# First MLP of a fused attention and MLP kernel: the products with w_ch2 two tiles behind those with w_ch1 instead of one

## Chip, cores and metric

One core of one Trainium2 chip. The metric is the device time of one execution in microseconds (us), the median of three runs. TensorE is called PE in the views, its weight loads PEld, VectorE DVE, ScalarE ACT, GpSimd POOL; SP is the engine that issues most transfers.

## What is computed

Three stages follow each other, all in float32 on the outside. Batch 4, 8 heads, 576 positions, head width 64, model width 512:

```python
def _attn_ref(q, k, v, f):
    ...
    decay = cum[:, :, :, None] - cum[:, :, None, :]
    scores = np.where(causal, -1000000000.0, scores + decay)
    ...
    return np.matmul(attn, v).astype(np.float32)

def _moe_ref(x, g_ln, w_ch1, w_ch2):
    ...
    xn = (x - mu) / np.sqrt(var + 1e-06) * g_ln
    ch = np.maximum(xn @ w_ch1, 0.0) @ w_ch2
    return (x + ch).astype(np.float32)

def _moe2_ref(x, w_in, w_spatial, b_spatial, w_out):
    h = np.maximum(x @ w_in, 0.0)
    ...
    return (gated @ w_out).astype(np.float32)
```

The middle one is the first MLP: 512 columns to 2048 with `w_ch1`, a relu, and back to 512 with `w_ch2`. Its normalisation is over the 512 columns.

## The kernel before

The 2304 rows (4 x 576) are cut into nine blocks of 256. Blocks 0 to 7 come from attention, one after the other; block 8 gathers the last 64 positions of each batch element. The first MLP works through eight groups, called 0 to 7 here: groups 0 to 6 have one block each, group 7 has blocks 7 and 8 together, so its matmuls are 512 columns wide where the others have 256. Attention of later blocks, the normalisation of the next block, the conversion of weights from 64-bit words (groups 0 and 1) and the loading of the second MLP's weights (group 7, `load_m2`) are written between the MLP's steps by a list of events sorted by due time in `run`; a list scheduler then fixes each engine's order by priority and readiness, and on the chip every engine runs its list in that order.

One step of a group is one tile `j` of 128 of the 2048 hidden columns (`NF` = 16 tiles). It has these parts:

- the **first products** (line 652), `w_ch1` times the normalised rows, into a PSUM tile `ph`. Weights and rows are split into a high and a low half in 16 bits, so there are 4 x 3 = 12 matmuls per tile (4 in group 0, which runs in float32). `ph` has **two** buffers;
- the relu in two halves: ScalarE writes `hh` (line 657), then VectorE `hl` from `ph` and `hh` (line 661). Both have three buffers. `ph` is free for tile `j` + 2 when both have read it;
- the **second products** (line 637, function `second`), `w_ch2` times `hh` and `hl`, again 12 matmuls, which accumulate over all 16 tiles in two PSUM banks `acc` (in group 7 two more, `s2`, which some views call `s`). They are issued one step late: step `j` issues the first products of tile `j` and then the second products of tile `j` - 1, which `pend` holds.

After the last tile `acc` is scaled by VectorE (line 677) and added to `x2_d` in memory by GpSimd's transfers (line 681).

In attention a pair of heads has its score products on line 280 (line 373 in blocks 2 and 3), is made into 16-bit probabilities `P` by VectorE and ScalarE, is transposed by transfers (line 303, queue of SP) into `PT`, and comes back to TensorE in 30 products `av` with the values (line 436; line 398 in blocks 2 and 3). The normalisation of a block has two small products with a matrix of ones (line 557): of the sum `ls` for the mean and of the squares `sq` for the variance. Behind them VectorE scales `xT` (line 587), and `split` makes `xh` (ScalarE, line 613) and `xl` (VectorE, line 614), the right sides of the first products.

Of the kernel before, what the change touches and what calls it, by code (L numbers as in the profile page):

```python
# [22 lines left out]
NF = DFF // P  # L23
# [12 lines left out]
NARROW = 4  # L36
W8 = 1
RAWB = 2

BLOCKS = [(0, 0), (2, 0), (0, 1), (2, 1), (0, 2), (1, 2), (2, 2), (3, 2)]  # L40
EPS = 1e-6
# [29 lines left out]
def f32(ap):  # L71
    return ap.bitcast(F32)
# [7 lines left out]
class Kernel:  # L80
# [140 lines left out]
    def vnorm(self):  # L221
# [4 lines left out]
        for b in range(B + 1):  # L226
            t = self.st.tile([P, 4, DM], F32, tag="raw", name="vraw", bufs=RAWB)
            if b < B:
# [261 lines left out]
    def load_raw(self, j):  # L490
        nc = self.nc
        cs = slice(j * P, (j + 1) * P)
        raw = self.raw[j] = self.st.tile([P, 2 * DM], I64, tag="raw", name="raw", bufs=RAWB)
        nc.sync.dma_start(out=raw[:, :DM].rearrange("p (k f) -> p k f", k=NK), in_=self.moe_w_ch1[:, cs].rearrange("(k p) f -> p k f", p=P))
# [104 lines left out]
    def mlp(self, g, states, y):  # L599
        nc, mo = self.nc, self.mo  # L600
        n = len(states)
        W = n * TOK
        if g:
            xn = [[mo.tile([P, 2 * TOK], F16, tag=tag, name=tag, bufs=MB["xh"]) for tag in ("xh", "xl")] for _ in range(NK)]

        def split(i):

            x, c = states[i](), slice(i * TOK, (i + 1) * TOK)
            for t in range(NK):
                with self.tc.high_priority(1):  # L610
                    if g:
                        scale, (xh, xl) = self.gs[:, t : t + 1], xn[t]
                        nc.scalar.activation(xh[:, c], x[:, t, :], AF.Copy, scale=scale)  # L613
                        nc.vector.scalar_tensor_tensor(out=xl[:, c], in0=x[:, t, :], scalar=scale, in1=xh[:, c], op0=ALU.mult, op1=ALU.subtract)  # L614
                    else:
                        nc.scalar.activation(x[:, t, :], x[:, t, :], AF.Copy, scale=self.gT[:, t : t + 1])
            return x

        acc = self.accs(W)
        clear, seen = {}, set()  # L620

        def weight(j, c0, right):

            cs = slice(c0, c0 + P)
            if not g:
                return [(self.wt[:, j + 2, cs], right)]
            h, l = self.pair(j)
            rh, rl = right
            return [(l[:, cs], rh), (h[:, cs], rl), (h[:, cs], rh)]

        def second(j, hidden, last):
            for m in range(NK):

                bank = m if n > 1 else m // 2
                terms = weight(j, DM + m * P, hidden)
                for e, (a, b) in enumerate(terms):
                    ins = nc.tensor.matmul(acc[m], lhsT=a, rhs=b, start=bank not in clear, stop=last and e == len(terms) - 1, skip_group_check=True)  # L637
                    if bank not in clear:
                        clear[bank] = ins
                    elif m not in seen and not e:  # L640
                        self.after(ins, clear[bank])
                    seen.add(m)

        pend = None
        for i in range(n):
            x = split(i)
        for j in range(NF):
            ph = self.bank("ph")[:, :W]
            for k in range(NK):
                terms = weight(j, k * P, (xn[k][0][:, :W], xn[k][1][:, :W]) if g else x[:, k, :])  # L650
                for e, (a, b) in enumerate(terms):
                    nc.tensor.matmul(ph, lhsT=a, rhs=b, start=k == e == 0, stop=k == NK - 1 and e == len(terms) - 1)  # L652
            hh = mo.tile([P, 2 * TOK], F16, tag="hh", name="hh", bufs=MB["hh"])
            hl = mo.tile([P, 2 * TOK], F16, tag="hl", name="hl", bufs=MB["hh"])[:, :W] if g else None
            hh = hh[:, :W] if g else f32(hh)
            with self.tc.high_priority(1):
                relu = nc.scalar.activation(hh, ph, AF.Relu)  # L657
                if g < 2:
                    self.done.append(relu)
                if g:  # L660
                    nc.vector.scalar_tensor_tensor(out=hl, in0=ph, scalar=0.0, in1=hh, op0=ALU.max, op1=ALU.subtract)  # L661
            if pend is not None:
                second(*pend)
            pend = (j, (hh, hl) if g else hh, j == NF - 1)
            yield
        second(*pend)
        c = GROUPS[g][0] * TOK
        for i in reversed(range(n)):

            t = mo.tile([P, NK, TOK], F32, tag="xT", name="t", bufs=MB["xT"])  # L670
            for m in range(NK):
                a = acc[m][:, i * TOK : (i + 1) * TOK]
                with self.tc.high_priority(1):
                    if n > 1 and m % 2:
                        nc.scalar.activation(t[:, m], a, AF.Copy, scale=self.und)
                    elif g:
                        nc.vector.tensor_scalar(out=t[:, m], in0=a, scalar1=self.und, scalar2=None, op0=ALU.mult)
                    else:
                        nc.vector.tensor_tensor(out=t[:, m], in0=y, in1=a, op=ALU.mult)  # L679

                nc.gpsimd.dma_start(out=self.x2_d[m * P : (m + 1) * P, c + i * TOK : c + (i + 1) * TOK], in_=t[:, m], accum_op=ALU.add)  # L681
        yield
# [499 lines left out]
```

## Time and profile before

| | us |
|---|---|
| median of three runs | 833.58 (832.38 to 833.69) |
| the profiled execution's own time | 839.44 |
| its span in the trace | 837.7 |

| engine | busy, us | share of the span |
|---|---|---|
| PE | 773.9 | 92% |
| PEld | 585.6 | 70% |
| DVE | 555.0 | 66% |
| ACT | 529.9 | 63% |
| POOL | 59.0 | 7% |

The span is what the trace covers; the execution's own time has what lies around it as well. Matmuls overlap each other in the pipeline, so the length given for one matmul is more than the distance to the next. "Idle before" is the time an engine stood still before a group of instructions, and the name behind the arrow is what ended it.

### The profile page before, as it was taken

What the parts mean: (1) busy time and instruction counts of PE and PEld (TensorE: products, weight loads), DVE (VectorE), ACT (ScalarE), POOL (GpSimd) and SP (SyncE); (2) the same over time, 40 slices, a digit from 0 to 9 for tenths busy, and PEclk for the clock granted to TensorE, in tenths of its full rate; (3) what the DMA queues carried; (4) which work ended last, traced back from release to release, by engine and by line L of the source; (5) the groups of instructions that cost most, each with busy time, mean ns of one, the idle gap of its engine ahead of it and who ended that gap; (6) DMA issues with size and microseconds to landing.
All of it is one profiled execution on the core that took longest, in us unless ns stands there. A gap on an engine that the chain in (4) does not pass through costs nothing.

```text
span 837.7 us, 16143 instructions
## 1 busy us (share of the span) xinstructions
PE 773.9 (92%) x5856; PEld 585.6 (70%) x5856; DVE 555.0 (66%) x1495; ACT 529.9 (63%) x1319; POOL 59.0 (7%) x87
## 2 busy tenths in 40 slices
PE   1799989889989999999999999699999999999997
PEld 1688877668877777787878788444446767768676
DVE  4556975788398879879777873768435464654734
ACT  4656874989288879867677772557325555646442
POOL 3000000100110101110101100200003000000000
PEclk9879999999999999999999999899999999999999
DMA  6557994765668896996697663643006220000101
GB/s 186 174 164 247 253 244 90 190 142 100 134 158 164 171 217 140 169 188 144 145 183 159 133 98 105 168 154 101 0 1 120 64 93 22 29 29 2 58 1 57
DMA packets 166066, 104.71 MB, mean 125 GB/s; under 512 B 106402, under 2 KB 153634, under 8 KB 165988
## 3 DMA queue, kind: packets, MB, share of 16 engines
q1 hardware_dynamic: 159800, 97.19, 47.9%
q0 software_dynamic: 5184, 4.72, 4.1%
q10 hardware_dynamic: 1004, 1.78, 0.6%
q8 instruction: 46, 0.75, 0.4%
q14 instruction: 32, 0.26, 0.1%
HBM read 64.37 MB, written 15.11 MB: 95 GB/s over the span
## 4 chain that ended last, share of the span: by engine, by line
PE 54%; DMA 15%; ACT 13%; DVE 11%; issue 4%; SPq 2%; POOL 0%; DVEq 0%; ACTq 0%; POOLq 0%
PE ph L652 11%; PE acc L637 10%; PE pb L593 7%; PE pb L594 7%; PE pb L595 7%; DMA PT<-P 5%; DMA raw<-in_moe_w_ch_dram 4%; PE av L436 2%; PE s L637 2%; DVE P L301 2%; DMA x_d<-xT 2%; DMA qk<-in_qk_dram 2%; ACT wt L546 1%; ACT sd L288 1%; PE s L280 1%
## 5 line engine op out<-in xcount | busy, mean ns | idle before, releaser
L637 PE MATMUL acc<-hh,wt 128*128 128x256 f16 (+2 forms) x960 | 200.2, 297 | 8.0 <-ACT hh L657 7.0
L652 PE MATMUL ph<-xh,wt 128*128 128x256 f16 (+1 forms) x896 | 189.1, 292 | 4.2 <-ACT xh L613 4.2
L637 PEld LDWEIGHTS <-wt 128*128 128x128 f16 x1344 | 127.9, 99 | 59.4 <-issue 19.8
L652 PEld LDWEIGHTS <-wt 128*128 128x128 f16 x1344 | 130.5, 99 | 49.7 <-issue 11.9
L652 PE MATMUL ph<-xl,wt 128*128 128x256 f16 (+1 forms) x448 | 131.0, 292 | 1.2 <-DVE xl L614 1.2
L637 PE MATMUL acc<-hl,wt 128*128 128x256 f16 (+1 forms) x416 | 114.4, 283 | 5.8 <-DVE hl L661 5.8
L245 ACT ACTIVATE P<-sd,st 128x512 f16<-128x512 f32 (+1 forms) x128 | 71.5, 587 | 31.9 <-DMA PT<-P 15.4
L657 ACT ACTIVATE hh<-ph 128x256 f16<-128x256 f32 (+2 forms) x128 | 50.9, 399 | 51.9 <-PE ph L652 51.7
L301 DVE SCALAR_TENSOR_TENSOR P<-sd,st,P 128x384 f16<-128x384 f32 (+1 forms) x96 | 59.7, 635 | 30.6 <-ACT P L245 30.5
L661 DVE SCALAR_TENSOR_TENSOR hl<-ph,hh 128x256 f16<-128x256 f32 (+1 forms) x112 | 50.6, 453 | 40.4 <-ACT hh L657 39.9
L280 PE MATMUL s<-x 68*128 68x384 f32 (+7 forms) x256 | 60.4, 355 | 2.6 <-ACT sq L573 1.0
L288 ACT ACTIVATE sd<-sd,st 128x384 f32<-128x384 f32 (+2 forms) x80 | 54.6, 682 | 8.7 <-DVE st L284 8.5
L681 POOL DMA_DIRECT2D x_d<-t x36 | 32.2, 1079 | 309.7 <-DVE t L679 146.3
L284 DVE CUSTOM_DVE_ANT_0 sd<-s,mask 128x384 f32<-128x384 f32 (+2 forms) x80 | 45.7, 580 | 5.2 <-PE s L280 4.5
L245 ACT ACTIVATE x<-qk 64x320 fp32r<-64x320 f32 (+1 forms) x64 | 41.0, 698 | 4.8 <-DMA qk<-in_qk_dram 3.9
L280 PEld LDWEIGHTS s<-x 68*128 68x128 f32 (+3 forms) x256 | 38.1, 177 | 7.9 <-PE s L280 1.3
L436 PE MATMUL av<-PT,vp 128*64 128x320 f16 (+2 forms) x480 | 34.3, 270 | 6.2 <-DMA PT<-P 6.2
L932 DVE SCALAR_TENSOR_TENSOR u<-pb,wsc,u 128x288 f32<-128x288 f32 x32 | 15.9, 513 | 33.3 <-PE pb L931 31.7
L593 PE MATMUL pb<-x2h,wil 128*128 128x288 f16 (+2 forms) x144 | 37.8, 273 | 0.0
L595 PE MATMUL pb<-x2h,wih 128*128 128x288 f16 (+2 forms) x144 | 37.8, 273 | 0.0
L594 PE MATMUL pb<-x2l,wih 128*128 128x288 f16 (+2 forms) x144 | 37.8, 273 | 0.0
L593 PE MATMUL pb<-wsh,vl 128*128 128x288 f16 x128 | 36.6, 286 | 0.2 <-DVE x2s L198 0.2
(266 smaller groups left out, 1608.3 us busy)
## 6 DMA issues: line engine op xcount, KB each, us to landing
raw<-in_moe_w_ch_dram SPq DMA_DIRECT2D x32, 512.0 KB
qk<-in_qk_dram SPq DMA_DIRECT2D x32, 448.0 KB
vraw<-in_v_dram SPq DMA_DIRECT2D x5, 1024.0 KB
vr<-in_v_dram SPq DMA_DIRECT2D x16, 320.0 KB
x_d<-xT SPq DMA_DIRECT2D x9, 512.0 KB
x_d<-t POOLq DMA_DIRECT2D x36, 128.0 KB, 5.7
out_dram<-o SPq DMA_DIRECT2D x32, 144.0 KB
raw<-in_moe_w_in_dram SPq DMA_DIRECT2D x8, 512.0 KB
```

The costliest lines, as they stand in the source:

```text
L245: self.nc.scalar.activation(out, in_, AF.Copy, scale=scale)
L280: nc.tensor.matmul(ps[: R * u + R, : c1 - c0], lhsT=x[:, lo - q0 - R * u : hi - q0], rhs=y[:, c0:c1], start=g == 0, stop=g == len(heads[u] ...
L288: nc.scalar.activation(sd[:M, :N], sd[:M, :N], AF.Exp, bias=st[:M, n : n + 1], scale=-1.0, accum_out=st[:M, 2:3])
L301: nc.vector.scalar_tensor_tensor(out=dl, in0=src, scalar=rs, in1=dh, op0=ALU.mult, op1=ALU.subtract)
L436: nc.tensor.matmul(pav[us, n0:W], lhsT=vp[:kr, vi, kt, us], rhs=heads[u][1][:kr, 2 * kt + pi, n0:W], start=(kt == 0 and (vi, pi) == (0, 1) ...
L593: first = mm(out, lhsT=al, rhs=bh, start=start, stop=False, **kw)
L594: mm(out, lhsT=ah, rhs=bl, start=False, stop=False, **kw)
L595: mm(out, lhsT=ah, rhs=bh, start=False, stop=stop, **kw)
L637: ins = nc.tensor.matmul(acc[m], lhsT=a, rhs=b, start=bank not in clear, stop=last and e == len(terms) - 1, skip_group_check=True)
L652: nc.tensor.matmul(ph, lhsT=a, rhs=b, start=k == e == 0, stop=k == NK - 1 and e == len(terms) - 1)
L657: relu = nc.scalar.activation(hh, ph, AF.Relu)
L661: nc.vector.scalar_tensor_tensor(out=hl, in0=ph, scalar=0.0, in1=hh, op0=ALU.max, op1=ALU.subtract)
```

## The change

`pend` becomes a list, and step `j` issues the second products of tile `j` - 2. The last two tiles' second products follow after the loop. Nothing is added or removed: on TensorE both programs have the same number of instructions. Lines behind the new constant stand one further down (653 for 652, 638 for 637, 658 for 657), and those behind the loop two (676 and on).

```diff
+AHEAD = 2
...
-        pend = None
+        pend = []
...
-            if pend is not None:
-                second(*pend)
-            pend = (j, (hh, hl) if g else hh, j == NF - 1)
+            pend.append((j, (hh, hl) if g else hh, j == NF - 1))
+            if j >= AHEAD:
+                second(*pend[j - AHEAD])
             yield
-        second(*pend)
+        for args in pend[-AHEAD:]:
+            second(*args)
```

What it does to the order on the engines is seen at three places.

TensorE in group 6, behind the last first product of tile 8 (`ph_6823` before, `ph_6811` now). Before, the second products of tile 7 (`hh_6785`) follow:

```order
L652 LDWEIGHTS wt_146
L652 MATMUL ph_6823<-xh_6349,wt_146 128x256
L637 LDWEIGHTS wt_146
L637 MATMUL acc_6351<-hh_6785,wt_146 128x256
L637 LDWEIGHTS wt_146
L637 MATMUL acc_6352<-hh_6785,wt_146 128x256
```

```order
L653 LDWEIGHTS wt_146
L653 MATMUL ph_6811<-xh_6349,wt_146 128x256
L638 LDWEIGHTS wt_146
L638 MATMUL acc_6351<-hh_6711,wt_146 128x256
L638 LDWEIGHTS wt_146
L638 MATMUL acc_6351<-hl_6712,wt_146 128x256
```

Now it is those of tile 6 (`hh_6711`), whose relu has had one tile more of time.

TensorE at the end of group 6, around the product for the mean of block 8 (`av<-ls`). Before, it stands in the middle of the first products of tile 15 (`ph_7051`), and 30 matmuls of the MLP follow it before the product of block 8's squares, behind which group 7 begins:

```order
L652 MATMUL ph_7051<-xl_6346,wt_146 128x256
L652 LDWEIGHTS wt_146
L652 MATMUL ph_7051<-xh_6345,wt_146 128x256
L557 MATMUL av_6858<-ls_6852,onesf_60 128x256
L652 LDWEIGHTS wt_146
L652 MATMUL ph_7051<-xh_6347,wt_146 128x256
```

```order
L653 MATMUL ph_7010<-xl_6350,wt_146 128x256
L653 LDWEIGHTS wt_146
L653 MATMUL ph_7010<-xh_6349,wt_146 128x256
L558 MATMUL av_6846<-ls_6840,onesf_60 128x256
L638 LDWEIGHTS wt_146
L638 MATMUL acc_6351<-hh_6965,wt_146 128x256
```

Now it follows tile 14's first products (`ph_7010`), and the second products of tile 12 (`hh_6965`), the whole of tile 15's first products and the second ones of tiles 13, 14 and 15 come after it: 60 matmuls.

ScalarE in group 7, up to the relu of tile 4 (`hh_7302` before, `hh_7290` now). Between the relus stand conversions of the second MLP's weights:

```order
L804 ACTIVATE spare_7514,wss_7511<-wsr_7510 128x576
L703 ACTIVATE wih_7181,ss_7410<-win_7180 128x512
L804 ACTIVATE spare_7514,wss_7511<-wsr_7510 128x576
L714 ACTIVATE wih_7181<-win_7180,win0_7270 128x512 x4
L475 ACTIVATE wor_7632<-raw8_7635 128x512
L804 ACTIVATE spare_7514,wss_7511<-wsr_7510 128x576
L657 ACTIVATE hh_7302<-ph_7289 128x512
```

```order
L476 ACTIVATE win_7168<-raw8_7357 128x512
L802 DMA spare_7501<-in_moe2_b_spatial_dram 1x576
L803 DMA spare_7501<-in_moe2_b_spatial_dram 1x576
L705 ACTIVATE wih_7169,ss_7398<-win_7168 128x512
L806 ACTIVATE spare_7502,wss_7499<-wsr_7498 128x576 x3
L705 ACTIVATE wih_7169,ss_7398<-win_7168 128x512
L806 ACTIVATE spare_7502,wss_7499<-wsr_7498 128x576
L658 ACTIVATE hh_7290<-ph_7277 128x512
L716 ACTIVATE wih_7169<-win_7168,win0_7258 128x512 x4
```

The relu now stands ahead of the four conversions `wih` by `win0` (714 before, 716 now) and of the first `wor`; the last raw copy of `win` (475, now 476) has six activations between it and the relu where there were 14, among them the relu of tile 3, which has moved ahead of that copy.

## Rows read from the trace of the kernel before

**Rows 1.** The page: busy time and share of the span of TensorE
```profile
PE 773.9 (92%) x5856; PEld 585.6 (70%) x5856; DVE 555.0 (66%) x1495; ACT 529.9 (63%) x1319; POOL 59.0 (7%) x87
```

**Rows 2.** Three stretches: length, then busy us (instructions) of PE, PEld, DVE, ACT, POOL, PEclk, DMA
```profile
142.00:179.00 37.00, 30.43 (x217) 23.71 (x217) 29.04 (x71) 36.64 (x74) 3.73 (x4) 0.92 0.53 138
300.00:530.00 230.00, 222.83 (x2025) 185.12 (x2026) 171.99 (x457) 162.38 (x410) 22.15 (x32) 1.00 0.73 146
530.00:580.00 50.00, 39.81 (x176) 17.79 (x173) 36.25 (x79) 30.61 (x65) 6.33 (x7) 0.93 0.58 177
```

**Rows 3.** TensorE's waits, 142 to 180 us: total, times, longest
```profile
PE acc L637 <- ACT hh L657: 2.8, 3, 1.3
PE acc L637 <- DVE hl L661: 1.1, 2, 0.6
```

**Rows 4.** TensorE's waits, 180 to 300 us
```profile
PE acc L637 <- ACT hh L657: 1.3, 1, 1.3
PE acc L637 <- DVE hl L661: 0.3, 1, 0.3
```

**Rows 5.** TensorE's waits, 300 to 530 us
```profile
PE av L436 <- DMA PT<-P: 4.8, 4, 1.8
PE acc L637 <- DVE hl L661: 2.3, 3, 1.1
...
PE acc L637 <- ACT hh L657: 0.6, 1, 0.6
```

**Rows 6.** TensorE's waits, 538 to 580 us (group 7)
```profile
PE acc L637 <- ACT hh L657: 2.4, 2, 1.6
...
PE acc L637 <- DVE hl L661: 0.8, 2, 0.4
```

**Rows 7.** The chain that ended last: start, length, what
```profile
225.89 8.10 DMA vr<-in_v_dram
246.32 6.16 DMA PT<-P
267.25 3.37 DMA PT<-P
...
495.46 1.80 PE av L436 x28
...
498.68 1.55 PE s L280 x10
...
574.98 2.59 PE ph L652 x12
```

**Rows 8.** TensorE in order of time at the end of group 6: start, length, [idle before]
```profile
521.12 0.27 PE L652 MATMUL ph<-xh,wt 128*128 128x256 f16 x1
521.23 0.27 PE L652 MATMUL ph<-xl,wt 128*128 128x256 f16 x1
...
527.45 0.60 PE L557 MATMUL av<-ls,onesf 128*128 128x256 f32 x2
...
531.47 0.27 PE L637 MATMUL acc<-hl,wt 128*128 128x256 f16 x1 [1.24 <-DVE hl L661]
...
533.06 0.70 PE L557 MATMUL av<-sq,onesf 128*128 128x256 f32 x2 [0.34 <-POOL sq L578]
537.95 0.59 PE L652 MATMUL ph<-xh,wt 128*128 128x512 f16 x2 [4.19 <-ACT xh L613]
```

**Rows 9.** ScalarE in order of time, group 7
```profile
562.08 0.66 ACT L475 ACTIVATE win<-raw 128x512 f32<-128x512 f32 x1 [1.47 <-DMA raw<-in_moe_w_in_dram]
...
562.69 0.63 ACT L703 ACTIVATE wih<-win 128x512 f16<-128x512 f32 x1
...
563.32 0.67 ACT L804 ACTIVATE spare<-wsr 128x576 f32<-128x576 f32 x1
...
563.98 0.58 ACT L657 ACTIVATE hh<-ph 128x512 f16<-128x512 f32 x1
...
571.60 0.58 ACT L657 ACTIVATE hh<-ph 128x512 f16<-128x512 f32 x1
```

**Rows 10.** TensorE in order of time: first second products of group 7
```profile
547.22 0.59 PE L637 MATMUL acc<-hh,wt 128*128 128x512 f16 x2
```

**Rows 11.** Stretches of 5 us at the start of group 7: length, PE busy (matmuls), PEclk, DMA
```profile
535.00:540.00 5.00, 0.85 (x3) 0.85 1.09 307
540.00:545.00 5.00, 5.00 (x13) 0.50 1.01 275
545.00:550.00 5.00, 5.00 (x24) 0.97 0.58 180
```

## The prediction

> **What bounds the kernel now.** I read the page first: TensorE is busy for 773.9 us, 92% of the span, and no other engine has more than 66% [rows 1]. That is one number for stages with different limits, so I next read the busy times by stretch. From 300 to 530 us TensorE works 222.8 of 230 us while VectorE and ScalarE have a quarter of their time free: there TensorE sets the pace. From 142 to 179 us ScalarE works 36.64 of 37.0 us, making the 16-bit weights: there ScalarE does. From 530 to 580 us no engine is full [rows 2]; that is a stretch of chains.
>
> Then I read what TensorE waits for, stretch by stretch. The waits that this change is about are those of the second products (`acc`, line 637) for the relu's halves `hh` and `hl`. They are 2.8 + 1.1 = 3.9 us in the stretch of ScalarE [rows 3], 1.3 + 0.3 = 1.6 us up to 300 us [rows 4], 2.3 + 0.6 = 2.9 us from there to 530 us [rows 5], and 2.4 + 0.8 = 3.2 us in group 7 [rows 6]. Add the 1.24 us at the end of group 6 [rows 8], and all of it is 12.8 us, 1.5% of the span. What each piece is worth depends on its stretch. Last I read the chain that ended last: from 226 to 300 us it runs through transfers, `vr` with 8.1 us and transposed probabilities `PT` with 6.2 and 3.4 us [rows 7], and hardly through TensorE.
>
> **The change, part by part.** Nothing is added, so all of it is in what stands where.
>
> *The steady step.* Successive first products start 0.11 us apart (521.12 and 521.23) [rows 8]. Before, between the last first product of tile j and the first second product of it stand 24 matmuls: 2.6 us for the relu. Now the second products of j are 24 further back, but the first products of tile j + 2 need the buffer `ph` of tile j, of which there are two, so the first who waits for `hl` of tile j comes after 36 matmuls: 3.9 us. The step gives 1.3 us more, not 2.6. From 300 to 530 us the longest wait for `hl` is 1.1 us and the one for `hh` 0.6 us [rows 5], so 1.3 us hides them all, and TensorE is what sets the pace: **-2.9 us** (between -2.9 and 0).
>
> *Stretch of ScalarE.* The same cover would hide its 3.9 us [rows 3], but the relus stand there in the queue of an engine that is idle for 0.36 us in 37 [rows 2], and this work does not shrink. TensorE would come sooner and wait later. I take that idle time, **-0.4 us** (between -3.9 and 0).
>
> *180 to 300 us.* 1.6 us [rows 4] beside a chain of transfers [rows 7]. A third of it, since TensorE enters the next stretch with some work done ahead: **-0.6 us** (between -1.6 and 0).
>
> *End of group 6.* TensorE stands idle for 1.24 + 0.34 + 4.19 us there. The last of it waits for `xh` of block 8, at the end of a chain that begins with the product for block 8's mean at 527.45 and ends at 537.95: 10.5 us through VectorE, ScalarE and GpSimd [rows 8]. Before, 30 matmuls of the MLP lie beside that chain; now it is 60, since the mean's product stands 30 matmuls earlier in TensorE's list. The chain begins 30 x 0.11 us sooner, and nothing in it becomes longer: **-3.3 us** (between -5.8, all of the idle time, and 0). What is late next is the same chain, by the 2.5 us that remain.
>
> *Group 7.* The last wait is for the relu of tile 4, which starts at 571.60. Now only six activations lie between the raw copy that starts at 562.08 and that relu. By the distances in the view (copy 0.61, `wih` 0.63, `spare` 0.66) it can start at 562.08 + 0.61 + 2 x 0.63 + 4 x 0.66 = 566.6 [rows 9]. TensorE must by then be through the first products up to tile 5 and the second ones up to tile 3. It begins the second ones at 547.22 [rows 10], with tiles 0 and 1 of the first done, and a batch of twelve takes 2.59 us [rows 7]: 547.22 + 8 x 2.59 = 567.9. So tile 4's relu is no longer late, and up to the 3.2 us of waits [rows 6] could go. I keep 0.9 us for waits on the way, since tiles 2 and 3 need `ph` back from relus that sit behind copies waiting for transfers: **-2.3 us** (between -3.2 and 0). All of group 7 moves with its start, the transfers of the weights too.
>
> *What attention loses.* The scheduler has also moved attention's products. Before, 111 and 140 matmuls stand between the last score product of head pairs 8 and 9 (the first two of block 6) and their first `av`; now 87 and 99. Pair 8 loses 14 of the MLP and 10 scores, 14 x 0.11 + 10 x 0.155 = 3.1 us; pair 9 loses 30 `av`, 6 of the MLP and 5 scores, 30 x 0.064 + 6 x 0.11 + 5 x 0.155 = 3.3 us (ten scores take 1.55 us, 28 `av` 1.80 us [rows 7]). Beneath runs the path score, VectorE, ScalarE, transpose, whose length I take as unchanged. Pairs 12 and 13 gain 29 and 54 matmuls. How much slack there was no view shows, so the bounds are +6.4 (both were just in time) and -4.8 (all waits for `PT` in this stretch go [rows 5]). Nearer the middle, a third of the upper end: **+2.0 us**.
>
> *What costs nothing.* `hh` and `hl` have three buffers, and the relu of tile j + 3 must now wait for the second products of tile j; in the new order these end at least twelve matmuls (1.3 us) before that tile's first products do, so no relu waits for a buffer; without those twelve it would, by the rest. On the queue of SP transposes and loads change places by a few positions around the pairs; every transpose's wait is in the attention term. GpSimd's additions of `x2_d` start with the group's end and nobody in groups 1 to 7 waits for them.
>
> **Sum**: -2.9 - 0.4 - 0.6 - 3.3 - 2.3 + 2.0 = -7.5 us against the profiled execution's own 839.44 us, so 831.9. That execution is 5.86 us over the median of the three runs; the same step from 833.58 gives **826.1 us**. Some 0.2% (1.7 us) is what a measurement of this kernel can tell from no change.
>
> **The rivals.** *The wait moves to `ph`.* If the relus are late because VectorE and ScalarE are late, and not by a fixed time behind the product, the wait for `acc` comes back as a wait for `ph`, two tiles on. Against it: no row has TensorE waiting for `ph` because of `hl` now, and VectorE works 172 of 230 us [rows 2, 5]. For it: the two buffers, and the longest wait, 1.6 us in group 7 [rows 6], is more than the new cover. Then the steady step and group 7 give nothing; -3.3 + 2.0 remains, 832.3 us, no change. The Trainium skill, in "Perfetto Trace Analysis", section "Optimization Strategy", says that the same gap repeating on an engine that should be full can mean too little PSUM for the next tile. By that rule two `ph` buffers would be the limit and this rival the outcome; the trace does not agree so far, since the waits stand at the reader of `hh` and `hl`, not at the writer of `ph`.
>
> *Attention sets the pace* (slower). The first scores of pairs 0 and 1 stand 12 and 24 MLP matmuls later in TensorE's list, those of pairs 7, 9 and 10 by 20 to 24. If the path from scores to `av` and not TensorE is the bound from 230 to 530 us, as the chain is to 300 us [rows 7], the start of it slips by 24 x 0.11 = 2.6 us, pairs 8 and 9 add 6.4 us, nothing of the removed waits comes back, and the earlier mean is eaten. Only group 7's -2.3 is left: +6.7 us, 840.3 us. It decides from the point where the two pairs together have less than 3 us of slack. Against it: 7 us of idle TensorE in 230 [rows 2].
>
> *The clock holds.* Behind the 4.19 us of idle time the granted clock was 0.50 from 540 to 545 us, the lower of the two levels (1.2 GHz), and 13 matmuls ran where the next 5 us had 24 [rows 11]: 13 x (5/13 - 5/24) = 2.3 us. If the shorter gap of about 2.5 us leaves the clock at 2.4 GHz, these come on top: 823.8 us. The skill's "TensorE: Matmul & The Clock Gate", section "Why this matters for your kernels", has only longer gaps between bursts of matmuls bring the clock down; the fall behind 4.19 us agrees, and no row here shows a gap of 2.5 us.
>
> **How the numbers follow.** The sum 0.58, the clock 0.08, the wait moved 0.13, attention 0.21. So faster 0.66, same 0.13, slower 0.21. The range begins where every gain is full but ScalarE's, the clock holds and attention loses nothing: -2.9 - 0.4 - 1.6 - 3.3 - 3.2 - 2.3 = -13.7, 819.9, rounded to 819; it ends at 839, short of the slower rival's full price. Of the likeliest case alone the range is 820 to 832.
>
> **What would show it.** Right: from 300 to 530 us hardly any wait of `acc` for `hh` or `hl`; the wait for `xh` before group 7 nearer 1 than 4 us; group 7's waits under 1 us, none for tile 4's relu. Wrong: TensorE waiting at `ph` for `hl`; over 5 us more of waits at `av` for `PT`, at pairs 8 and 9 above all. The forecast falls if waits from 300 to 530 us grow as a whole.

## The result and the profile after

The change takes 820.92 us (median of four executions, 817.55 to 822.35), the kernel before 833.63 us beside it: ratio 0.9843, 95% interval 0.9809 to 0.9877, so 10 to 16 us less. Forecast were 826.1 us, range 819 to 839, faster with a chance of 0.66. Direction and range held; of the gain only 7.5 of some 13 us were forecast, three terms of the sum were wrong and one was missing.

The two profiled executions are 21.9 us apart (839.44 and 817.55), because the one of before lies above its median and that of the change below. Where a difference between traces is read below, a second profile of before (run 1, 834.18 us) therefore stands beside the first.

The page of the change, busy time and share of the span, against [rows 1]:

```profile
PE 763.3 (94%) x5856; PEld 578.6 (71%) x5856; DVE 554.3 (68%) x1495; ACT 527.5 (65%) x1319; POOL 57.9 (7%) x87
```

TensorE's waits of the change from 142 to 180 us (total, times, longest), against [rows 3]:

```profile
PE acc L638 <- ACT hh L658: 4.2, 2, 2.6
PE ph L653 <- DVE hl L662: 1.2, 2, 0.7
```

From 300 to 515 us, where group 6 ends now, against [rows 5]:

```profile
PE av L437 <- DMA PT<-P: 2.4, 4, 0.8
PE s L281 <- ACT x L246: 1.0, 1, 1.0
PE s L281 <- DVE st L292: 0.8, 1, 0.8
PE s L281 <- ACT st L291: 0.3, 1, 0.3
```

And from 515 to 570 us, the end of group 6 and group 7, against [rows 6, 8]:

```profile
PE ph L653 <- ACT xh L614: 4.2, 1, 4.2
PE ph L653 <- DVE hl L662: 0.9, 1, 0.9
PE ph L653 <- DVE xl L615: 0.8, 1, 0.8
```

Three readings. From 300 us on no second product waits for `hh` or `hl` any more. In group 7 the same holds, and one wait of 0.9 us for `hl` has come up at `ph`. But the 4.2 us for `xh` before group 7, from which the forecast took 3.3, are all still there; and in the stretch of ScalarE the waits are no shorter, 5.4 us against 3.9, although groups 0 and 1 are where most of the time was won, as the runs show.

### The profile page after: what moved, and what is told of

It reads as the page before. It is cut to its first block, busy times and chain, and to the rows that moved or that the text cites. A ratio compares the mean times of both kernels' runs of the same rounds, so it can differ in the third digit from the quotient of the medians.

```text
span 815.8 us, 16121 instructions
## 1 busy us (share of the span) xinstructions
PE 763.3 (94%) x5856; PEld 578.6 (71%) x5856; DVE 554.3 (68%) x1495; ACT 527.5 (65%) x1319; POOL 57.9 (7%) x87
## 4 chain that ended last, share of the span: by engine, by line
PE 60%; DMA 15%; ACT 11%; DVE 9%; issue 3%; SPq 1%; ACTq 0%; DVEq 0%
PE ph L653 13%; PE acc L638 12%; PE pb L594 8%; PE pb L595 8%; PE pb L596 8%; DMA PT<-P 5%; DMA raw<-in_moe_w_ch_dram 4%; PE s L281 3%; PE av L437 3%; DVE P L302 2%; ACT x L246 2%; PE s L638 1%; DMA raw<-in_moe_w_in_dram 1%; ACT wt L547 1%; DMA qk<-in_qk_dram 1%
## 5 line engine op out<-in xcount | busy, mean ns | idle before, releaser
L638 PE MATMUL acc<-hl,wt 128*128 128x256 f16 (+1 forms) x416 | 116.1, 283 | 0.0
L281 PE MATMUL s<-x 68*128 68x384 f32 (+7 forms) x256 | 62.1, 358 | 5.7 <-DVE hl L662 2.3
```

The costliest lines, as they stand in the source:

```text
L281: nc.tensor.matmul(ps[: R * u + R, : c1 - c0], lhsT=x[:, lo - q0 - R * u : hi - q0], rhs=y[:, c0:c1], start=g == 0, stop=g == len(heads[u] ...
```

## The experiments

All runs are compared with the kernel before in the same rounds on the same chip. The group numbers say in which groups the second products run two tiles behind.

| run | what | median, us | ratio to before (95%) |
|---|---|---|---|
| 1 | before again | 834.76 | 1.0030 (1.0002 to 1.0059) |
| 2 | groups 0 and 1 | 825.20 | 0.9906 (0.9869 to 0.9943) |
| 3 | groups 2 to 6 | 828.72 | 0.9931 (0.9894 to 0.9967) |
| 4 | group 7 | 831.77 | 0.9976 (0.9938 to 1.0015) |
| 5 | the change again | 821.03 | 0.9838 (0.9798 to 0.9878) |
| 6 | group 0 | 826.79 | 0.9886 (0.9845 to 0.9927) |
| 7 | group 1 | 832.01 | 0.9945 (0.9911 to 0.9978) |
| 8 | the change, own bank for block 8's mean | 812.49 | 0.9733 (0.9697 to 0.9769) |
| 9 | before, own bank | 830.65 | 0.9948 (0.9915 to 0.9981) |
| 10 | own bank, three tiles behind | 808.49 | 0.9694 (0.9642 to 0.9746) |
| 11 | own bank, four tiles behind | 810.11 | 0.9721 (0.9656 to 0.9787) |

Run 1 has the same program on both sides and is 0.3% off, with an interval that just leaves out 1: 0.2% is less than these medians can tell, and the intervals are rather too narrow than too wide.

### Run 1: before again

> The kernel before, unchanged, a second time. Up to 62 us both profiled programs have the same order of instructions on TensorE, yet the profile of before begins the first product of group 0 at 62.32 us and that of the change at 56.73: in before a wait of 2.25 us for qk at 34 us is followed by a granted clock of 0.50 from 40 to 50 us. Theory A (this fall belongs to that one execution): the time is 833.6 within 0.2%, the new profile has no fall there, group 0 begins near 57 us, and of the 21.9 us between the two profiles some 6 were never the change's. Theory B (the fall belongs to the order of before): it is there again, group 0 begins near 62 us.

Measured: 834.76 us against 834.30. The new profile begins group 0 at 57.41 us, and the fall is gone. TensorE's granted clock by slice (each a fortieth of the span, tenths of full speed), of run 1:

```profile
PEclk9999999899999999999999999899999999999999
```

In the first profile of before the second and third slices read 8 and 7, and the stretch from 40 to 50 us had 0.50. Theory A holds: some 5 of the 21.9 us between the two profiles belong to one execution.

### Runs 2, 3 and 4: the change in some groups only

```diff
-AHEAD = 2
+AHEAD = (2, 2, 1, 1, 1, 1, 1, 1)
...
-            if j >= AHEAD:
-                second(*pend[j - AHEAD])
+            if j >= AHEAD[g]:
+                second(*pend[j - AHEAD[g]])
...
-        for args in pend[-AHEAD:]:
+        for args in pend[-AHEAD[g] :]:
```

and `(1, 1, 2, 2, 2, 2, 2, 1)` in run 3, `(1, 1, 1, 1, 1, 1, 1, 2)` in run 4.

> Second products two tiles behind in groups 0 and 1 only, one tile behind in groups 2 to 7. Theory A (the gain lies where relus are late, in the stretch of ScalarE and in group 7): between the profiles groups 0 and 1 took 8.6 us less, a good part of it granted clock; so 4 to 6 us of the 12.7 us, near 828.5. Theory B (as predicted: the stretch of ScalarE gives 0.4 us, the gain lies in the steady step, the end of group 6 and group 7): 833 or so, no change by 0.2%.

> Two tiles behind in groups 2 to 6 only. Prediction: steady step -2.9, 180 to 300 us half of -0.6, end of group 6 -3.3, attention +2.0, so 829. Theory A (from the two profiles: from the end of group 2 to the end of group 6 the change took 1.3 us more, not less; attention has taken all of the gain, and the idle time of 4.2 us before group 7 is the chain behind block 8's variance product, which is left as it was): within 2 us of 833.6, with the 4.2 us wait for xh still there and hardly a wait for hh or hl from 300 to 530 us.

> Two tiles behind in group 7 only; up to there the order on TensorE is that of before, instruction for instruction, and attention's part stays as it was. Prediction: -2.3 us of waits (0 to -3.2). Theory A (from the two profiles, group 7 took 4.0 us less from its first product to its last, of which some 1 us clock): 829.5 to 831.5. Theory B (it is the wait that moves on, to the loads of the second MLP's weights): 833.6, no change.

Measured by the ratios, of 834.3 us: groups 0 and 1 -7.8 us (-10.9 to -4.8), groups 2 to 6 -5.8 (-8.8 to -2.8), group 7 -2.0 (-5.2 to +1.3, so not certain by the times alone). The sum, -15.6, agrees with the whole, -13, within these intervals.

So groups 2 to 6 came out as the prediction had them (829), group 7's -2.3 lies in an interval that reaches over 0, and Theory A of run 3, which gave groups 2 to 6 nothing, fell. It had been read from the first two profiles, in which attention's matmuls lie otherwise in the groups: in run 2 and in the change alike, 1055 of TensorE's matmuls lie between the first product of group 0 and the last of group 1, where before there were 1078. TensorE's waits of run 3 in groups 2 to 6 (212.56 to 518.64 us):

```profile
PE av L437 <- DMA PT<-P: 4.3, 4, 1.8
PE s L281 <- DVE x L264: 1.3, 3, 0.5
PE s L281 <- DMA x<-decay_d: 0.9, 1, 0.9
PE s L281 <- PE s L281: 0.8, 1, 0.8
PE ph L653 <- DVE hl L662: 0.3, 1, 0.3
```

and of run 1 in the same groups (212.85 to 527.86 us):

```profile
PE av L436 <- DMA PT<-P: 4.3, 5, 1.7
PE acc L637 <- DVE hl L661: 3.8, 5, 1.2
PE s L280 <- ACT sq L573: 1.7, 1, 1.7
PE s L280 <- DVE x L263: 0.7, 1, 0.7
PE acc L637 <- ACT hh L657: 0.6, 1, 0.6
...
```

The 4.4 us at `acc` are gone, 0.3 us have come back at `ph`, `av` waits for `PT` as long as in run 1, and the waits at the scores (`s`) are 3.0 us in all where they were 3.8: what the scheduler moved in attention has added no waiting here.

Group 7 of run 4, in which TensorE's list up to there is that of before (waits from 538 to 626 us):

```profile
PE ph L653 <- DVE hl L662: 0.8, 1, 0.8
PE ph L653 <- DVE xl L615: 0.8, 1, 0.8
```

against, in run 1 (534 to 626 us):

```profile
PE acc L637 <- ACT hh L657: 2.9, 3, 1.6
PE ph L652 <- DVE xl L614: 0.9, 1, 0.9
PE acc L637 <- DVE hl L661: 0.8, 2, 0.4
```

3.7 us at `acc` become 0.8 at `ph`. But these waits also change while group 7 stays one tile behind: at `acc` they are 2.4 us in run 2 and 1.9 in run 3, and in run 7, described below, nothing is left there (533 to 622 us):

```profile
PE ph L653 <- ACT xh L614: 4.1, 1, 4.1
PE ph L653 <- DVE xl L615: 0.4, 1, 0.4
```

From its first product to its last second product group 7 takes 91.8 and 92.7 us in the two profiles of before, 90.0, 89.5 and 87.1 in runs 2, 3 and 7, and, two tiles behind, 88.9 in run 4 and 87.8 in the change. So the wait moves as forecast, but that group 7 gains time is not shown, neither by the times nor by the traces.

### Runs 5, 6 and 7: why groups 0 and 1

Run 2 had been forecast at no change, so the question was what the prediction had wrong there. Runs 6 and 7 are `(2, 1, 1, 1, 1, 1, 1, 1)` and `(1, 2, 1, 1, 1, 1, 1, 1)` in the diff above; run 5 is the change.

> The change, unchanged, on the same chip and in the same rounds as the three below. Expected 820.9 within 2 us and, against before, 12 to 14 us. The three parts measured so far (groups 0 and 1: -9.1, groups 2 to 6: -5.6, group 7: -2.5) add up to -17.2 us. Theory A (the parts overlap: with groups 0 and 1 changed, some matmuls of attention slide out of the stretch of ScalarE into groups 2 to 6 and cost there what the steady step saves): the whole stays at -13. Theory B (the parts add and the earlier sessions differed): -17.

> Two tiles behind in group 0 only. In the profiles, counted from the first product of group 0, ScalarE begins to make the 16-bit weights at 78.8 to 81.0 us where group 0 runs one tile behind, and at 76.2 to 76.8 where it runs two behind. Theory A (half of the gain of groups 0 and 1 is this earlier start, and everything behind it moves along): -3.5 us, 831. Theory B (TensorE's idle time in group 1 is what counted): no change, 834.

> Two tiles behind in group 1 only. Theory A (TensorE stands idle some 8.5 us for hh, hl and attention while ScalarE makes the weights, and is then full for 40 us until the end of group 1, so what it does early in the stretch of ScalarE it need not do later): -4 us or so, 830. Theory B, that of the prediction (the work of ScalarE does not shrink, TensorE would come sooner and wait later): -0.4 us, 834.

Measured: the change -13.5 us again (0.9838 of 835.4); group 1 alone -4.6 (-7.4 to -1.8), where the prediction's reasoning said -0.4; group 0 alone -9.5 (-12.9 to -6.1). For run 5 that is Theory A, and the traces fit it: in groups 2 to 6 TensorE has 23 matmuls more in the change than in run 3, and they take 310.9 us (309.0 in run 5) where run 3 took 306.1.

Run 7 decides against that reasoning, and the windows say in part how. Cut at the points where ScalarE begins and ends the 16-bit weights, and at the end of group 1: length, busy us (instructions) of PE, PEld, DVE, ACT, POOL, PEclk, DMA share, GB/s. Run 1:

```profile
136.25:172.03 35.78, 30.21 (x214) 24.00 (x213) 27.85 (x61) 35.78 (x72) 3.73 (x4) 0.90 0.55 143
172.03:212.85 40.82, 39.35 (x373) 32.49 (x372) 27.98 (x92) 27.22 (x89) 2.27 (x2) 1.00 0.59 118
```

Run 7:

```profile
139.53:177.40 37.87, 30.54 (x232) 25.00 (x231) 29.96 (x67) 36.54 (x74) 3.73 (x4) 1.00 0.60 153
177.40:214.07 36.67, 36.67 (x343) 30.07 (x342) 26.51 (x87) 26.27 (x86) 2.12 (x3) 0.95 0.57 112
```

The change:

```profile
132.93:170.55 37.62, 32.09 (x248) 26.65 (x248) 28.06 (x62) 36.77 (x73) 3.72 (x4) 0.95 0.59 154
170.55:205.84 35.29, 35.29 (x334) 29.45 (x332) 28.27 (x91) 26.02 (x86) 2.18 (x2) 1.00 0.53 118
```

ScalarE's stretch has not become shorter, but is 35.78, 37.87 and 37.62 us long: in that the prediction was right. TensorE's idle time in it has not become shorter either: 5.57 us (not the 8.5 that run 7's expectation names), 7.33 and 5.53. But TensorE gets 214, 232 and 248 matmuls done in it, and the next 40 us are a stretch in which TensorE hardly stops (39.35 of 40.82 us before). What it did early, it need not do there: 373, 343 and 334 matmuls remain, and 40.82 us become 36.67 and 35.29. The two stretches together: 76.6 us before, 74.5 in run 7, 72.9 in the change.

The granted clock differs between the three (0.90, 1.00 and 0.95 in ScalarE's stretch), but it does not set the number of matmuls: run 4, which has group 1 as before, gets the same 214 done in 35.79 us at 0.95. Two other things are mixed in. Of the 34 matmuls more in the change, 18 lay ahead of the stretch before (8 second products of group 0 and 10 `av`), and 23 matmuls (11 in run 7) have left groups 0 and 1 for later groups. So it is shown that TensorE gets more done beside ScalarE and has less to do behind it; how much of that comes from the later wait for the relu, and how much from what else the scheduler moved, is not.

Group 0's part is ahead of that stretch and in it. From the last product `gram` (the one on which the weights' scales rest) to the first 16-bit weight, TensorE is busy all the time in both; run 1:

```profile
124.10:136.25 12.15, 12.15 (x81) 10.15 (x78) 5.90 (x28) 6.25 (x21) 0.00 (x0) 1.00 0.52 111
```

and the change:

```profile
122.07:132.93 10.86, 10.86 (x66) 9.06 (x65) 5.27 (x26) 5.51 (x21) 0.00 (x0) 1.00 0.45 67
```

Here 15 fewer matmuls stand in TensorE's list, and ScalarE begins 1.3 us sooner. No second product of group 0 waited for `hh` in the two profiles of before, so this is the order alone. Counted from group 0's first product, ScalarE begins at 78.8 us in run 1 and at 76.2 in the change; the other 1.3 us of that lie ahead of the last `gram`, and what made them is open. From group 0's first product to group 1's last it is 155.4 us in run 1 and 149.1 in the change, 6.3 less, of which the two stretches are 3.7; run 2 has -7.8 by its times. Run 6 gave more than that, and its profiled execution is the longest of its six (836.14 us), so its trace does not tell why; that groups 0 and 1 alone add up to -14.1 where both together gave -7.8 (all with some 3 us to either side) stays open.

### Runs 8 and 9: the wait before group 7

In `norm` and `mean`, for block 8 alone, a bank of the scores in place of `av`:

```diff
-        pm = self.bank("av")[:, :TOK]
+        pm = self.bank(tag)[:, :TOK]
...
-            pm = self.mean(s)
+            pm = self.mean(s, tag=tag)
...
-            pv = self.mean(sq[:, 0])
+            pv = self.mean(sq[:, 0], tag=tag)
...
-            g = self.norm(xT, s, y, g > 0)
+            g = self.norm(xT, s, y, g > 0, "s2" if n == last else "av")
```

> The change, and block 8's mean and variance get a PSUM bank of the scores (idle by then) where they shared the one bank av with block 7's. The product of the mean then stands some 95 and that of the variance some 45 matmuls earlier in TensorE's list. Theory A (the idle 4.2 us before group 7 is the chain of 4.8 us behind the variance product, which in before and in the change alike comes last in group 6; 45 matmuls are 4.9 us and cover it): the wait for xh before group 7 falls below 1 us, the granted clock does not fall there, and the time is 4 to 7 us below the change alone. Theory B, that of the prediction (the chain starts at the mean's product, and its length is what counts): the mean's product stood 30 matmuls earlier in the change and the wait stayed 4.2 us, so it would have to stay again. Theory C (group 7's weights, loaded behind the last blocks, are the bound): the 4.2 us come back as a wait further on, no change.

First what the change itself left, TensorE in order of time at the end of group 6 (start, length, what, [idle before]):

```profile
509.85 0.60 PE L558 MATMUL av<-ls,onesf 128*128 128x256 f32 x2
...
516.72 0.27 PE L638 MATMUL acc<-hh,wt 128*128 128x256 f16 x1
516.83 0.60 PE L558 MATMUL av<-sq,onesf 128*128 128x256 f32 x2
521.61 1.01 PE L653 MATMUL ph<-xh,wt 128*128 128x512 f16 x2 [4.18 <-ACT xh L614]
```

and GpSimd, which makes the squares' sum:

```profile
514.62 0.79 POOL L579 TENSOR_TENSOR sq<-sq 128x256 f32<-128x256 f32 x1
```

The mean's product did move ahead, with all 60 matmuls behind it, and the squares were ready at 514.62 + 0.79 = 515.41. But the product that takes them is on TensorE too, last in the list, and waits its turn until 516.83. From there 4.8 us of VectorE and ScalarE remain, as before (533.06 to 537.95, 4.9 us [rows 8]). From the mean's product to group 7 it is 11.8 us, where it was 10.5 [rows 8]. Only the 1.24 us for `hl` and the 0.34 us for `sq` have gone.

Run 8, the same place:

```profile
514.01 0.60 PE L558 MATMUL s<-sq,onesf 128*128 128x256 f32 x2
519.58 0.59 PE L653 MATMUL ph<-xh,wt 128*128 128x512 f16 x2
521.11 0.38 PE L653 MATMUL ph<-xl,wt 128*128 128x512 f16 x1 [0.94 <-DVE xl L615]
```

with the windows of run 8:

```profile
520.00:525.00 5.00, 4.05 (x20) 1.76 (x19) 2.25 (x6) 0.74 (x3) 2.59 (x3) 1.00 1.08 294
525.00:530.00 5.00, 5.00 (x25) 2.29 (x24) 2.67 (x6) 4.51 (x7) 0.88 (x1) 1.00 0.67 169
```

against those of the change:

```profile
520.00:525.00 5.00, 2.60 (x6) 0.80 (x6) 5.00 (x11) 1.91 (x5) 0.94 (x2) 0.50 1.10 311
525.00:530.00 5.00, 5.00 (x20) 2.10 (x19) 1.76 (x4) 3.90 (x7) 0.00 (x0) 0.81 1.02 309
```

The wait for `xh` is gone, the granted clock (the third number from the end) stays at 1.00 where it read 0.50 and 0.81, and the time is 812.49 against 821.03 us in the same rounds. Theory A holds. The wait, 4.2 us, and what the clock took from TensorE's busy time in the two windows, 2.60 x 0.50 + 5.00 x 0.19 = 2.3 us, come to 6.5 of the 8.5 us; the rest is within the intervals. The edit moves both products, so it does not say what each of them is worth; that the mean's alone is not enough is what the change shows.

> Block 8's mean and variance in a bank of their own, second products one tile behind in all groups as before. Theory A (the 4.2 us before group 7 and the fall of the granted clock behind them hang on the bank av alone and have nothing to do with how far the second products are behind): 7 to 9 us below before, 826 to 828, and the change's own gain is the same 13 to 14 us with the bank as without. Theory B (the change's longer tail of second products is what covers the chain, so the bank needs it): 2 to 4 us below before.

Measured: 0.9948, -4.3 us (-7.1 to -1.6), between the two theories and nearer B. In its trace the variance product stands at 523.27 us and group 7 begins at 530.97, with 3.5 us of idle time for `xh` left: with one tile behind, fewer second products come after it. In the 5 us from 530 the clock reads 0.66, and then 1.00. So by the waits the bank needs the longer tail of second products; by the times bank and change together (run 8, -22.3 us) give 4.5 us more than each alone (-4.3 and -13.5), which is within the intervals.

### Runs 10 and 11: further behind

```diff
-AHEAD = 2
+AHEAD = 3
...
-MB = dict(xT=4, xh=8, hh=3, y=2)
+MB = dict(xT=4, xh=8, hh=4, y=2)
```

(4 and `hh=5` in run 11), both with block 8's own bank.

> As the run with block 8's own bank, with the second products three tiles behind and four buffers for hh and hl. Theory A (two buffers of ph let the first products of tile j + 2 wait for hl of tile j whatever is done with the second ones, so a third tile adds no cover; what is left of waits is for ph and for the transfers of attention): within 2 us of 812.5. Theory B (late relus still cost where ScalarE is full, and more work put behind them hides it): 2 to 4 us less.

> As the run with block 8's own bank, with the second products four tiles behind and five buffers for hh and hl. Three tiles behind had given 808.5 against 812.5 with two, by less idle TensorE before and while ScalarE makes the weights. Theory A (the cover counts where ScalarE is late, and three tiles, some 4 to 5 us more, hide all but the waits for ph and for the weights): within 2 us of 808.5. Theory B (more ahead is more done in the stretch of ScalarE): 805 or less. Theory C (attention's products slide back too far, its chain becomes late): over 812.

Measured: 0.9694 and 0.9721 against run 8's 0.9733. Run 10 has the lowest median, 808.49 us, but its interval reaches over run 8's. What the intervals show is that both beat the kernel before and the change. That a third tile is worth anything is not shown, so none of the theories is decided; these runs have more buffers as well.

## Why the prediction was right, and where it was wrong

- **Steady step, and 180 to 300 us: right.** Forecast -2.9 and -0.6. All waits of `acc` from group 2 to the end of group 6 went and 0.3 us came back at `ph`; without the end of group 6 that is 2.9 us by run 1 and 4.1 by the first profile of before. That such waits count in full where TensorE sets the pace agrees with run 3 (-5.8 us, with the end of group 6), whose interval is wide.
- **Attention: wrong by its size.** Forecast +2.0 between -4.8 and +6.4, without a row for the slack. Run 3 has the waits of `av` for `PT` unchanged, 4.3 us. Of the two pairs named, the change's first `av` of pair 8 waits 0.5 us (at 373.50 us), that of pair 9 not at all: all but 0.5 us of the 24 and 41 matmuls taken away had been slack. The change itself has one wait that run 3 has not, 2.3 us of a score product between 205 and 300 us (1.7 in run 5), but `av` waits 1.1 us less for `PT` in groups 2 to 6.
- **End of group 6: wrong.** Forecast -3.3, measured -1.6 by the waits. The step that failed is "the chain begins 30 x 0.11 us sooner, and nothing in it becomes longer". The chain became 1.3 us longer (11.8 for 10.5 us), because it passes through TensorE a second time: the variance product stands behind the 60 matmuls that were counted as cover for the whole chain, and waits 1.4 us for its turn (515.41 to 516.83). They cover the chain's first half and nothing of the 4.8 us behind that product. Run 8 shows it from the other side. The errors of attention and of this term, +2.0 and -1.7, have opposite signs and nearly cancel: that groups 2 to 6 came out right as a sum is luck.
- **Groups 0 and 1: wrong, and the largest error.** Forecast -0.4 for the stretch of ScalarE, with -3.9 as the other end; measured -7.8 for both groups. The step that failed is "TensorE would come sooner and wait later". Run 7 gives -4.6 us for group 1 alone: TensorE is idle in that stretch at least as long as before, but it gets more done there, and behind it TensorE is the bound, so that it has less left to do. The rows for that were in the trace of before: TensorE works 39.8 of the 40 us from 180 to 220. How much of it the relu's cover is worth stays open, as said above.
- **The start of that stretch: left out.** The forecast priced waits only; that the new order also lets the weights' scales be ready sooner (15 matmuls, 1.3 us) had no term.
- **Group 7: the wait moved as forecast, the gain is not shown.** Forecast -2.3. The relu of tile 4 starts 26.5 us after the group's first product (548.10 us) where it was 33.7 [rows 8, 9]; forecast were 28.7. 3.7 us at `acc` became 0.8 at `ph` in run 4, but the time of run 4 is -2.0 us with an interval over 0, and in run 7 the waits of `acc` went with group 7 left one tile behind.
- **The rivals.** *The wait moves to `ph`* happened for 0.9 us in group 7, 1.2 us in the stretch of ScalarE and 0.3 us behind it, nowhere else. *Attention sets the pace* did not. *The clock holds* did not either: the gap stayed 4.2 us and the clock fell to 0.50 behind it; with the gap gone, in run 8, it did not fall. Its price, 2.3 us, is what run 8 bears out; but a gap of 2.5 us need not have held the clock, as the last section shows.

In all, the direction came out right because the gain that was missed, in groups 0 and 1, has the same sign as the rest, and the time lies within the range because the range is wide.

## What to carry to other kernels

A stretch in which another engine is full can still be worth filling: look at the next stretch, and if your engine is full there, work that it gets done early is work that it need not do there. When a chain between engines is said to have cover on one of them, mark every point at which it comes back to that engine: cover counts from the last of these points, and work put ahead of it holds the chain up. And before costing a reorder of one loop, ask which other work the scheduler lets pass it.

## What was not expected of the hardware

Executions of one program differ more than the first few showed: 35 executions of before in one session lie between 827.24 and 841.33 us, and their mean granted clock between 0.991 and 0.973. By a straight line through all runs here, each kernel with its own mean, 0.01 of mean clock goes with 6 to 7 us. The clock also fell behind waits much shorter than the one before group 7. In run 1, TensorE waits for the relu in the stretch of ScalarE (length and PEclk as above):

```profile
160.00:165.00 5.00, 4.47 (x25) 2.91 (x26) 3.06 (x6) 5.00 (x14) 0.00 (x0) 0.66 0.32 58
```

The longest wait there, 1.6 us for `hh`, ends at 160.0 us. The Trainium skill, in "TensorE: Matmul & The Clock Gate", section "Why this matters for your kernels", has longer gaps between bursts of matmuls bring the clock down; the 4.2 us before group 7 agree. That section does not cover the fall in this stretch, behind waits of 1.6 us and less.
